# Numerators of a linear attention as 64-column products, with sums moved behind the transposes

## The chip, the core and the metric

One Trainium2 chip, one of its cores. The metric is the device time of one execution in microseconds. The kernel before took 926.39 us (median of three runs, 924.83 to 926.86). The profile that is read below is one execution of 926.11 us.

## What is computed

The reference is a FAVOR attention (4 batches, 8 heads, 576 tokens, head size 64, 128 features) followed by two feed-forward blocks on its 2304 x 512 output:

```
phi(x) = exp(x @ omega.T - |x|^2/2 - max) / sqrt(128)      # x = q or k, scaled
kv  = einsum('bhsm,bhsd->bhmd', phi(k), v)
z   = sum over tokens of phi(k)
num = einsum('bhsm,bhmd->bhsd', phi(q), kv)
den = einsum('bhsm,bhm->bhs', phi(q), z) + 1e-6
x   = num / den, heads side by side            # (2304, 512)
x   = silu(x @ w_in) @ w_out
out = (silu(x @ w_gate) * (x @ w_val)) @ w_out2
```

Everything is float32. The change touches only the attention.

## The kernel before

**Units and steps.** The attention runs over 8 units. A unit is a pair of heads and two batches, 1152 tokens in 9 chunks of 128. Each chunk is a step, so there are 72 steps and two more that finish. Two batches of 576 tokens meet inside chunk 4 of each unit: its first 64 tokens belong to one batch and its last 64 to the other.

**What a step does.** In step s, `proj` (L755 to L757) makes the features of chunk s+1 for k and q in six products of 256 columns, in one of five PSUM banks that are used in turn (`bank`). `soft` takes the maxima on VectorE (L765) and four exponentials on ScalarE (L769, tile `kq`). `kv_tr` works on the chunk of two steps ago (`LAG = 2`): it adds phi(k).T @ [v, 1] into the sums of the batch (L789, one product of 65 columns for each head), and transposes phi(q) on TensorE (L805), which ScalarE copies to `qp` (L816).

**Numerators.** When a batch's sums are complete, VectorE copies them to `st` (L826). Numerators are made for groups of three chunks (`num`, L843): for each chunk and head, one product whose weights are 128 columns of `qp` (the tokens) and whose moving operand is `st` (65 columns: the numerator and its denominator). In chunk 4 the 128 tokens belong to two batches, so that chunk already is done as products of 64 weight columns, first two for the lower half of the partitions and then two for the upper half. VectorE divides (L855 to L858), TensorE transposes the result (L868), VectorE copies it out (L877).

**When.** `tail` sets numerators two and six steps after the sums end: with u the unit, group 0 in step 9u+8, group 1 in 9u+12, group 2 in 9u+16. In step 70 there are two groups. The last two groups are made by `last_nums` when the feed-forward phase has begun. That is 24 calls: 20 in steps of their own, 2 in step 70, 2 in `last_nums`.

**Order of the work.** Every engine works through its instructions in the order in which the program issues them. Between the steps' own work, `feed` puts operations that prepare the feed-forward phase: weights of double precision turned into float32 pairs (`conv`), and operands split into high and low parts (`x`). Its choice depends on step numbers, not on times. So VectorE, ScalarE and GpSimd have a fixed list of work for each step. A projection waits until the exponentials that read its bank last are done, and `kv_tr` waits for the exponentials of its chunk.

A float32 product shows in the trace as two weight loads and two matmuls; a product of `fp32r` operands as one each.

Of the kernel before, what the change touches and what calls it, by code (L numbers as in the profile page):

```python
# [42 lines left out]
def kernel(  # L43
# [13 lines left out]
    nc = tc.nc  # L57
    ctx.enter_context(tc.manual_schedule())
    P = 128
    DM, NT = outT.shape  # L60
    D, M = omT.shape
# [12 lines left out]
    VH = D + 1  # L74
# [594 lines left out]
    def bank():  # L669
        rot.append(rot.pop(0))  # L670
        return ps[rot[-1]].rearrange("p (a b) -> p a b", a=2)
# [10 lines left out]
    raw, hl, kq, qp, kvps = {}, {}, {}, {}, {}  # L682
    v_t = [vp.tile([P, NCH, VW], F32, name=f"v{i}") for i in range(2)]
# [8 lines left out]
    def runs(lo, hi):  # L692
        for b in range(lo // S, (hi - 1) // S + 1):
            a, z = max(lo, b * S), min(hi, (b + 1) * S)
            yield b, a - lo, z - lo, a == b * S, z == (b + 1) * S
# [83 lines left out]
    def kv_tr(s):  # L779
        u, c = divmod(s, NCH)  # L780
        e = kq[s]
        ended = []
        for b, a, z, first, last in runs(c * P, (c + 1) * P):
            if first:
                kvps[u, b] = px.popleft()
            acc = ps[kvps[u, b]]
            for h in range(2):
                o = h * VH
                nc.tensor.matmul(  # L789
                    acc[:, o : o + VH],  # L790
                    e[a:z, 0, h * M : (h + 1) * M],
                    v_t[u % 2][a:z, c, o : o + VH],
                    start=first and h == 0,
                    stop=last,
                    skip_group_check=True,
                )
            if last:
                ended.append(b)
        if c == 0:
            qp[u] = ap1.tile([P, 2, UT], F32, tag="qp", name="qp", bufs=2)  # L800
        if c % 2 == 0:
            tps[u] = bank()
        t = tps[u]
        for h in range(2):
            nc.tensor.transpose(  # L805
                t[:, h, (c % 2) * P : (c % 2 + 1) * P], e[:, 1, h * M : (h + 1) * M], ident
            )
        kq.pop(s)
        if c % 2 == 1 or c == NCH - 1:
            c0 = (c - c % 2) * P  # L810
            n = (c + 1) * P - c0
            o = qp[u][:, :, c0 : c0 + n]
            if False:
                dve_q.append(lambda: nc.vector.tensor_copy(o, t[:, :, :n]))
            else:
                act_q.append(lambda: nc.scalar.activation(o, t[:, :, :n], AF.Copy))  # L816
        return [(u, b) for b in ended]

    st = {}
# [15 lines left out]
    def num(u, g, to=None):  # L835

        pxs[u, g] = x = px.popleft() if to is None else to
        acc = ps[x]
        for c in range(g * GC, (g + 1) * GC):
            for b, a, z, _, _ in runs(c * P, (c + 1) * P):  # L840
                for h in range(2):
                    o = (c - g * GC) * VW + h * VH
                    nc.tensor.matmul(  # L843
                        acc[a:z, o : o + VH],
                        qp[u][:, h, c * P + a : c * P + z],
                        st[u, b][:, h * VH : (h + 1) * VH],
                        start=True,
                        stop=True,
                        skip_group_check=True,
                    )  # L850

    def divide(u, g):
        acc = ps[pxs[u, g]][:, : GC * VW].rearrange("p (c w) -> p c w", w=VW)
# [37 lines left out]
    later = {}  # L891
# [4 lines left out]
    def tail(u, b, s):  # L896
        if b and u == NU - 1:
            return
        for g, a in ((1, s + 2), (2, s + 6)) if b else ((0, s + 2 - (u == NU - 1)),):
            at(a, num, u, g)  # L900
            at(a, lambda g=g: dve_q.append(lambda: divide(u, g)))
            at(a + 2, turn, u, g)
            at(a + 2, lambda g=g: dve_q.append(lambda: take_out(u, g)))
            if g == GC - 1:
                at(a + 4, store, u)
# [5 lines left out]
    LAG = 2  # L911

    def step(s):
# [21 lines left out]
        if LAG <= s < NSTEP + LAG:  # L935
            for ub in kv_tr(s - LAG):
                kv_evac(*ub)
                tail(*ub, s)
# [55 lines left out]
    def last_nums():  # L994

        u = NU - 1
        num(u, 1, 7)
        num(u, 2, 6)
        divide(u, 1)
        divide(u, 2)  # L1000
        nc.scalar.activation(silu, silu, AF.Silu)
        clk["PE"] += 1.8
        clk["ACT"] = max(clk["ACT"], clk["PE"]) + 1.5
        clk["DVE"] = max(clk["DVE"], clk["PE"]) + 2.0
        actx.close()
        operands("rb")
        streams["x"].extend(to_come.pop(0)())
        later_on.append((5, lambda: last_turn(1)))
        later_on.append((7, lambda: last_turn(2)))
# [632 lines left out]
```

## Time and profile before

| | |
|---|---|
| median of three runs | 926.39 us |
| profiled execution, its own time | 926.11 us |
| its span, first to last instruction | 924.3 us |
| TensorE busy (matmul) | 905.0 us, 98% |
| VectorE busy | 657.7 us, 71% |
| ScalarE busy | 558.4 us, 60% |
| GpSimd busy | 197.0 us, 21% |
| attention: last step's products end | about 146 us |

The span is shared by the attention (to about 146 us) and the two feed-forward blocks. Busy shares over the whole span hide that the other engines are much fuller in the attention than later. Matmuls are pipelined and their modelled ends overlap, so the time that a stream of products takes is read from the distance of the starts of the weight loads (PEld), not from the duration of one.

### The profile page before, as it was taken

What the parts mean: (1) busy time and instruction counts of PE and PEld (TensorE: products, weight loads), DVE (VectorE), ACT (ScalarE), POOL (GpSimd) and SP (SyncE); (2) the same over time, 40 slices, a digit from 0 to 9 for tenths busy, and PEclk for the clock granted to TensorE, in tenths of its full rate; (3) what the DMA queues carried; (4) which work ended last, traced back from release to release, by engine and by line L of the source; (5) the groups of instructions that cost most, each with busy time, mean ns of one, the idle gap of its engine ahead of it and who ended that gap; (6) DMA issues with size and microseconds to landing.
All of it is one profiled execution on the core that took longest, in us unless ns stands there. A gap on an engine that the chain in (4) does not pass through costs nothing.

```text
span 924.3 us, 15768 instructions
## 1 busy us (share of the span) xinstructions
PE 905.0 (98%) x5591; PEld 895.3 (97%) x5591; DVE 657.7 (71%) x1055; ACT 558.4 (60%) x1190; POOL 197.0 (21%) x244
## 2 busy tenths in 40 slices
PE   8999999999999998999999999999999999999998
PEld 8999999999999998999999899999999999899998
DVE  4898986857574398586689899574747447968584
ACT  5788785876667675455457765554455447445453
POOL 6676951104343100000000014221303010000000
PEclk9999999999999999999999999999999999999999
DMA  7576515848989991715613755562626159371701
GB/s 218 183 235 208 174 50 197 271 157 275 317 291 358 349 382 58 232 55 163 206 43 109 244 164 187 174 201 79 213 68 222 47 184 314 114 240 52 237 16 69
DMA packets 109888, 169.94 MB, mean 184 GB/s; under 512 B 9200, under 2 KB 93808, under 8 KB 109808
## 3 DMA queue, kind: packets, MB, share of 16 engines
q1 hardware_dynamic: 108640, 168.33, 55.8%
q8 instruction: 44, 0.72, 0.3%
q10 hardware_dynamic: 1168, 0.59, 0.2%
q14 instruction: 36, 0.29, 0.1%
HBM read 107.02 MB, written 61.87 MB: 183 GB/s over the span
## 4 chain that ended last, share of the span: by engine, by line
PE 90%; DVE 4%; DMA 3%; ACT 2%; issue 1%; SPq 0%; DVEq 0%; ACTq 0%
PE ps L1066 43%; PE ps L1433 31%; PE ps L843 3%; PE ps L789 3%; PE ps L755 2%; PE ps L756 2%; PE ps L757 2%; PE ps L805 2%; DMA g_d<-fa 1%; PE ps L868 1%; DVE ra L1296 1%; DMA fa<-in_moe_w_in 1%; DVE ra L419 0%; DMA ra<-wu_val 0%; DVE fa L1124 0%
## 5 line engine op out<-in xcount | busy, mean ns | idle before, releaser
L376 POOL TENSOR_TENSOR fa<-fa 128x256 f32<-128x256 f32 x136 | 112.6, 841 | 529.0 <-DVE fa L357 301.3
L1066 PE MATMUL ps<-ra 128*128 128x384 f32 x840 | 156.3, 335 | 3.0 <-ACT ps L1083 3.0
L1066 PE MATMUL ps<-rb,ra 128*128 128x384 f32 x840 | 157.3, 340 | 0.0
L1066 PE MATMUL ps<-rc,ra 128*128 128x384 f32 x840 | 156.8, 339 | 0.0
L1066 PEld LDWEIGHTS ps<-ra 128*128 128x128 f32 x840 | 146.7, 188 | 4.3 <-ACT ps L1083 4.3
L1066 PEld LDWEIGHTS ps<-rb,ra 128*128 128x128 f32 x840 | 148.7, 188 | 0.3 <-ACT ps L1083 0.3
L1066 PEld LDWEIGHTS ps<-rc,ra 128*128 128x128 f32 x840 | 148.6, 188 | 0.1
L1083 ACT ACTIVATE ps<-ps 128x384 f32<-128x384 f32 x180 | 85.5, 476 | 88.7 <-PE ps L1066 82.1
L1140 DVE TENSOR_TENSOR fa<-fa,ps 128x384 f32<-128x384 f32 x120 | 66.2, 552 | 100.5 <-ACT ps L1083 78.1
L1292 ACT ACTIVATE ra<-fa 128x768 fp32r<-128x768 f32 x105 | 88.0, 844 | 81.2 <-PE ps L1433 64.4
L1296 DVE TENSOR_TENSOR ra<-fa,ra 128x768 fp32r<-128x768 f32 x105 | 100.5, 957 | 50.5 <-PE ps L1433 31.9
L1433 PE MATMUL ps<-ra,rb 128*128 128x384 f32 x720 | 129.4, 340 | 0.0
L1433 PEld LDWEIGHTS ps<-ra,rb 128*128 128x128 f32 x720 | 127.8, 189 | 0.8 <-DVE ra L1296 0.6
L1433 PE MATMUL ps<-ra 128*128 128x384 f32 x612 | 109.7, 337 | 6.7 <-DVE ra L1296 6.5
L1433 PEld LDWEIGHTS ps<-ra 128*128 128x128 f32 x612 | 106.7, 189 | 8.8 <-DVE ra L1296 8.0
L769 ACT ACTIVATE kq<-ps,nb 128x128 f32<-128x128 f32 x288 | 83.1, 403 | 25.3 <-DVE nb L765 24.1
L1433 PE MATMUL ps<-ra,rc 128*128 128x384 f32 x432 | 78.2, 340 | 1.6 <-DVE ra L1296 1.6
L1433 PEld LDWEIGHTS ps<-ra,rc 128*128 128x128 f32 x432 | 76.1, 188 | 2.7 <-DVE ra L1296 2.7
L1107 ACT ACTIVATE fa<-fa 128x384 f32<-128x384 f32 x84 | 43.8, 522 | 28.8 <-DVE fa L1140 28.5
L1316 DVE TENSOR_TENSOR fa<-ra,fa 128x768 f32<-128x768 f32 x63 | 60.1, 954 | 0.7
L1292 ACT ACTIVATE ra<-ra 128x768 fp32r<-128x768 f32 x42 | 35.5, 845 | 36.0 <-PE ps L1433 32.1
L1296 DVE TENSOR_TENSOR ra<-ra 128x768 fp32r<-128x768 f32 x42 | 40.2, 958 | 20.9 <-PE ps L1433 9.3
(100 smaller groups left out, 1227.6 us busy)
## 6 DMA issues: line engine op xcount, KB each, us to landing
g_d<-fa SPq DMA_DIRECT2D x168, 192.0 KB, 3.4
fa<-g_d SPq DMA_DIRECT2D x42, 384.0 KB, 4.4
ra<-g_d SPq DMA_DIRECT2D x42, 384.0 KB, 4.1
fa<-in_moe_w_out SPq DMA_DIRECT2D x28, 512.0 KB, 5.3
fa<-in_moe_w_in SPq DMA_DIRECT2D x16, 512.0 KB, 5.0
wd_out<-fa SPq DMA_DIRECT2D x14, 512.0 KB, 3.3
fa<-in_moe_w_gate SPq DMA_DIRECT2D x12, 512.0 KB, 3.9
fa<-in_moe_w_val SPq DMA_DIRECT2D x12, 512.0 KB, 5.2
```

The source lines that it names most:

```text
L376: f(blk(f"S{n}"), blk(l), blk(r))
L769: nc.scalar.activation(e[:, i, h * M : (h + 1) * M], ps[:, i, h * M : (h + 1) * M], AF.Exp, bias=nb[:, 2 * i + h : 2 * i + h + 1],)
L789: nc.tensor.matmul(acc[:, o : o + VH], e[a:z, 0, h * M : (h + 1) * M], v_t[u % 2][a:z, c, o : o + VH], start=first and h == 0, stop=last, ...
L843: nc.tensor.matmul(acc[a:z, o : o + VH], qp[u][:, h, c * P + a : c * P + z], st[u, b][:, h * VH : (h + 1) * VH], start=True, stop=True, sk ...
L1066: nc.tensor.matmul(ps[b][:, :N], cut(l, j * P, P), cut(r, j * N, N), start=start and c == 0, stop=stop and c == 5, skip_group_check=True,)
L1083: nc.scalar.activation(out() if callable(out) else out, src, AF.Copy)
L1107: nc.scalar.activation(b["t"], src, AF.Silu)
L1140: nc.vector.tensor_add(t, t if in_place else p5[n], ps[bank_][:, :N])
L1292: nc.scalar.activation(ops[s, p, k][0], src(), AF.Copy)
L1296: nc.vector.tensor_sub(l, src(), h.bitcast(F32))
L1316: (nc.gpsimd if eng == "POOL" else nc.vector).tensor_sub(z(PLACE[to]), z(PLACE.get(l, l)), z(PLACE.get(r, r)))
L1433: nc.tensor.matmul(ps[BANKS[p] + e][:, :N], cut(a, e * P, P), b, start=p in FIRST and i == 0 and c == 0, stop=p in LAST and i == fp - 1 an ...
```

## The change

In `num` each product of 128 weight columns becomes two of 64, one that writes the lower half of the partitions and one that writes the upper half. In those steps that make numerators, the sums of k and v (the same products as before, otherwise of 128 weight columns) are made in halves of 64 columns as well, and are issued after the transposes, directly ahead of the numerators. Steps without numerators keep their sums as they were, and `last_nums` changes through `num` alone.

```
@@ kv_tr
+        halves = any(f is num for f, _ in later.get(s + LAG, ()))
+        then = None
...
-            for h in range(2):
-                o = h * VH
-                nc.tensor.matmul(
-                    acc[:, o : o + VH],
-                    e[a:z, 0, h * M : (h + 1) * M],
-                    v_t[u % 2][a:z, c, o : o + VH],
...
+            def sums(w, a=a, z=z, first=first, last=last, acc=acc):
+                for h in range(2):
+                    o = h * VH
+                    for i in range(0, M, w):
+                        nc.tensor.matmul(
+                            acc[i : i + w, o : o + VH],
+                            e[a:z, 0, h * M + i : h * M + i + w],
+                            v_t[u % 2][a:z, c, o : o + VH],
...
+            if halves:
+                then = sums
+            else:
+                sums(M)
...            (the transposes)
+        if then:
+            then(D)
@@ num
                     o = (c - g * GC) * VW + h * VH
-                    nc.tensor.matmul(
-                        acc[a:z, o : o + VH],
-                        qp[u][:, h, c * P + a : c * P + z],
+                    for i in range(a, z, D):
+                        nc.tensor.matmul(
+                            acc[i : i + D, o : o + VH],
+                            qp[u][:, h, c * P + i : c * P + i + D],
```

TensorE, the first step with a group 0: `v` and `kq` are the sums' operands, `ident` those of the transposes, `st` and `qp` those of the numerators; each row is a product before it is taken apart into two instructions.

```order
-L789 MATMUL ps_84<-v_98,kq 128x65 x2
-L805 MATMUL ps_81<-ident,kq 128x128 x2
-L843 MATMUL ps_85<-st,qp 128x65 x6
+L814 MATMUL ps_81<-ident,kq 128x128 x2
+L793 MATMUL ps_84<-v_98,kq 64x65 x4
+L855 MATMUL ps_85<-st,qp 64x65 x12
```

The transposes stand first, and the eight products of 128 weight columns have become sixteen of 64 in one row.

TensorE, the first step with a group 1, which holds chunk 4; the two products of the next projection follow.

```order
-L789 MATMUL ps_83<-v_99,kq 128x65 x2
-L805 MATMUL ps_81<-ident,kq 128x128 x2
-L843 MATMUL ps_84<-st,qp 128x65 x2
-L843 MATMUL ps_84<-st,qp 64x65 x4
-L843 MATMUL ps_84<-st,qp 128x65 x2
+L814 MATMUL ps_81<-ident,kq 128x128 x2
+L793 MATMUL ps_83<-v_99,kq 64x65 x4
+L855 MATMUL ps_84<-st,qp 64x65 x12
 L755 MATMUL ps_78<-om_hi,hik 128x256
 L756 MATMUL ps_78<-om_hi,lok 128x256
```

Before, four products of 64 columns stood between products of 128; now all sixteen are of 64, and the step after begins as it did. On VectorE, ScalarE, GpSimd and the DMA queues the order is the same in both kernels.

## Rows read from the trace of the kernel before

**Rows 1.** The page's first part: busy us (share of the span) and instructions.

```profile
PE 905.0 (98%) x5591; PEld 895.3 (97%) x5591; DVE 657.7 (71%) x1055; ACT 558.4 (60%) x1190; POOL 197.0 (21%) x244
```

**Rows 2.** The chain of waits, 0 to 146 us, shares by line.

```profile
by line: PE ps L789 20.5%; PE ps L843 19.9%; PE ps L755 12.9%; PE ps L756 12.6%; PE ps L757 12.2%; PE ps L805 11.9%; PE ps L868 4.9%; DMA rawq<-in_q 2.8%; SPq L720 0.8%; DVE lok L708 0.6%; issue 0.3%; SPq L699 0.3%; PE ps L1043 0.1%; DVEq L
```

**Rows 3.** Timeline, weight loads from 72.8 us, a group 2: start us, us, what.

```profile
73.42 1.42 PEld L843 LDWEIGHTS ps<-st,qp 128*128 128x128 f32 x12
74.75 0.19 PEld L755 LDWEIGHTS ps<-om_hi,hik 128*128 128x128 f32 x1
```

**Rows 4.** Timeline, weight loads from 62.7 us, a group 1 with chunk 4.

```profile
63.34 1.50 PEld L843 LDWEIGHTS ps<-st,qp 128*128 128x128 f32 x16
64.76 0.19 PEld L755 LDWEIGHTS ps<-om_hi,hik 128*128 128x128 f32 x1
```

**Rows 5.** Groups by shape, weight loads, 0 to 150 us: count, busy us, mean ns, idle before.

```profile
L843 PEld LDWEIGHTS ps<-st,qp 128*128 128x128 f32 x256 | 31.0, 192 | 0.5
...
L843 PEld LDWEIGHTS ps<-st,qp 128*64 128x64 f32 x64 | 2.6, 136 | 0.5
```

**Rows 6.** Timeline, weight loads, 63.9 to 64.3 us: chunk 4 alone.

```profile
63.93 0.32 PEld L843 LDWEIGHTS ps<-st,qp 128*64 128x64 f32 x8
```

**Rows 7.** Timeline of weight loads from 146 us: the last numerators.

```profile
146.96 2.90 PEld L843 LDWEIGHTS ps<-st,qp 128*128 128x128 f32 x28
```

**Rows 8.** Windows of the attention: length, then busy us of PE, PEld, DVE, ACT, POOL.

```profile
30.30:79.50 49.20, 49.20 (x456) 48.32 (x454) 46.80 (x94) 39.36 (x127) 36.16 (x45) 1.00 0.60 185
79.50:104.30 24.80, 24.80 (x235) 24.12 (x233) 21.65 (x42) 19.93 (x66) 18.77 (x22) 1.00 0.68 218
104.30:146.00 41.70, 41.70 (x386) 41.02 (x385) 32.70 (x69) 32.17 (x106) 23.66 (x27) 1.00 0.26 81
```

**Rows 9.** A window from 91.94 us, the same columns as above.

```profile
91.94:104.27 12.33, 12.33 (x119) 11.99 (x117) 11.69 (x22) 9.63 (x31) 12.00 (x14) 1.00 0.50 147
```

**Rows 10.** Waits of VectorE, 30.3 to 79.5 us: total us, times, longest.

```profile
DVE rc L855 <- PE ps L843: 2.5, 4, 1.1
DVE fa L350 <- ACT fa L343: 0.2, 1, 0.2
```

**Rows 11.** Timeline of all engines from 78.0 us, two rows.

```profile
77.76 0.67 ACT L769 ACTIVATE kq<-ps,nb 128x128 f32<-128x128 f32 x2
...
79.42 0.37 PE L755 MATMUL ps<-om_hi,hik 128*128 128x256 f32 x1
```

**Rows 12.** Timeline of VectorE from 87.5 us; in brackets the idle time before.

```profile
87.94 0.43 DVE L350 TENSOR_SCALAR fa<-fa 128x512 uint32<-128x512 uint32 x1 [0.81 <-ACT fa L343]
...
89.75 0.16 DVE L855 TENSOR_SCALAR rc<-ps 128x6 f32<-128x6 f32 x1 [0.79 <-PE ps L843]
...
92.43 0.16 DVE L855 TENSOR_SCALAR rc<-ps 128x6 f32<-128x6 f32 x1 [0.49 <-PE ps L843]
```

**Rows 13.** Timeline of all engines from 103.8 us, two rows.

```profile
103.50 0.63 ACT L769 ACTIVATE kq<-ps,nb 128x128 f32<-128x128 f32 x2
...
104.27 0.36 PE L755 MATMUL ps<-om_hi,hik 128*128 128x256 f32 x1
```

**Rows 14.** Timeline of all engines from 130.5 us, two rows.

```profile
130.18 0.88 ACT L769 ACTIVATE kq<-ps,nb 128x128 f32<-128x128 f32 x3
...
131.72 0.36 PE L755 MATMUL ps<-om_hi,hik 128*128 128x256 f32 x1
```

**Rows 15.** Timeline of VectorE from 147 us: the last divisions.

```profile
148.70 0.17 DVE L855 TENSOR_SCALAR rc<-ps 128x6 f32<-128x6 f32 x1 [2.49 <-PE ps L843]
...
150.04 0.16 DVE L855 TENSOR_SCALAR rc<-ps 128x6 f32<-128x6 f32 x1 [0.36 <-PE ps L843]
...
150.47 0.56 DVE L858 TENSOR_TENSOR nt<-ps,rc 128x384 f32<-128x384 f32 x1
```

**Rows 16.** The chain of waits from 130 us, in order of time: its end.

```profile
156.42 6.09 DMA fa<-in_moe_w_in
...
164.03 96.12 PE ps L1066 x545
```

More of the change, by code (lines that the diff above doesn't have):

```diff
@@ L786, in kv_tr @@
             acc = ps[kvps[u, b]]
-            for h in range(2):
-                o = h * VH
-                nc.tensor.matmul(
-                    acc[:, o : o + VH],
-                    e[a:z, 0, h * M : (h + 1) * M],
-                    v_t[u % 2][a:z, c, o : o + VH],
[L793 to L796, printed above, removed]
+            def sums(w, a=a, z=z, first=first, last=last, acc=acc):
[6 more added lines that the diff above has]
+                            v_t[u % 2][a:z, c, o : o + VH],
+                            start=first and h == 0,
+                            stop=last,
+                            skip_group_check=True,
+                        )
+            if halves:
+                then = sums
+            else:
+                sums(M)
             if last:
@@ L842, in num @@
                     o = (c - g * GC) * VW + h * VH
-                    nc.tensor.matmul(
-                        acc[a:z, o : o + VH],
-                        qp[u][:, h, c * P + a : c * P + z],
[L846 to L850, printed above, removed]
+                    for i in range(a, z, D):
+                        nc.tensor.matmul(
+                            acc[i : i + D, o : o + VH],
+                            qp[u][:, h, c * P + i : c * P + i + D],
+                            st[u, b][:, h * VH : (h + 1) * VH],
+                            start=True,
+                            stop=True,
+                            skip_group_check=True,
+                        )
     def divide(u, g):
```

## The prediction, made before the changed kernel ran

> **What bounds the kernel now.** I read the page's first part, the chain of waits over the attention, the weight loads of TensorE by shape and in time, and the windows of the attention for the other engines. Over the whole span TensorE is busy 98% of the time and the others at most 71% [rows 1]. In the first 146 us the chain lies on TensorE's lines almost alone: the sums (L789) hold 20.5% of it and the numerators (L843) 19.9%, each nearly twice a projection line [rows 2]. So what a step takes is what TensorE needs for it, and the question has two halves: how much shorter the changed products make TensorE's own work, and how long the other engines can follow.
>
> **TensorE's own work.** A product of 65 moving columns is paced by its weight load. In a step with a group 2, twelve instructions of 128 weight columns start at 73.42 and the next projection's load at 74.75 us [rows 3]: 1.33 / 12 = 0.111 us for each, sums included, since they have the same shape. A group 1 holds eight of these and the eight 64-column instructions of chunk 4, and takes 64.76 - 63.34 = 1.42 us [rows 4]; less 8 x 0.111 = 0.89, chunk 4 costs 0.53 us with everything around it. A load of 64 columns lasts 136 ns on average [rows 5], yet all eight are over in 0.32 us [rows 6]. One after another at the half of 0.111 us they would need 7 x 0.056 + 0.136 = 0.53 us. They go in pairs, one for each half of the partitions: (0.32 - 0.136) / 3 = 0.06 us from pair to pair. So a pair of halves, which does the work of one 128-column instruction, costs 0.06 instead of 0.111 us, and going into this shape and out of it costs 0.53 - 4 x 0.06 = 0.29 us once.
>
> This is where a rule speaks against the change. The Trainium skill, TensorE: Matmul & The Clock Gate, "The mechanism", says that a weight load overlaps matmuls in flight only when the row group differs; these halves use all rows, so they would gain nothing. The trace disagrees by rows 6. The Trainium skill, TensorEngine Tiling (Array Packing), "Key Properties", says that changing the tiling mode drains the engine but that tiles load and multiply in parallel; the 0.29 us and the pairs are what that looks like here.
>
> Step by step, with n instructions of 128 columns before and n pairs after, the block costs 0.29 + 0.06n:
> - Thirteen steps with a group 0 or 2: 12 numerators and 4 sums, 16 x 0.111 = 1.78 us before, 0.29 + 0.96 = 1.25 after. Gain 0.53 us each, 6.9 in sum. If the sums had stayed as 128 columns, the gain would be 0.32.
> - Seven steps with a group 1: (8 + 4) x 0.111 + 0.53 = 1.86 before, 1.25 after; 0.61 each, 4.3 in sum.
> - Step 70, with two groups: 28 x 0.111 = 3.11 before, 1.97 after; 1.14.
> - The last two groups, no sums: 20 x 0.111 + 0.53 = 2.75 (28 weight loads, busy 2.90 with the last one's tail [rows 7]), 1.73 after; 1.0.
>
> Together 13.3 us of TensorE's time; with 0.056 us for a pair it would be 14.3. The transposes that move ahead of the sums cost nothing: same instructions, and ScalarE gets them earlier. The sums of those steps are never the ones that end a batch, so their later place delays no copy.
>
> **How far the others follow.** The other engines keep their lists of work. From 30.3 to 79.5 us VectorE is busy 46.80 of 49.20 us, and GpSimd is busy 12.00 of 12.33 us later on [rows 8, 9]. VectorE's maxima feed the exponentials, and a projection must wait until those that read its bank are done. So TensorE can be ahead of its old schedule by no more than the exponentials' lead plus the slack that the old schedule had there. I call the gained time "lead" and follow it by stretches.
> - To 30.3 us: one group 0 and one group 1, lead 1.14 us. VectorE idles enough to follow.
> - To 79.4 us: TensorE would gain six of 0.53 and two of 0.61, to a lead of 5.5. VectorE can gain only what it idles. It waits for numerators 2.5 us, of which 1.1 is the wait that ends at the window's start, and 0.2 for ScalarE [rows 10]: 1.4 to 1.6, so its lead is 2.55 to 2.75. At 79.42 a projection starts 0.99 us after the exponentials of 77.76 + 0.67 end [rows 11]. TensorE's lead is cut to 2.75 + 0.99 = 3.75; 1.8 us are lost.
> - To 104.3 us: gains of 2 x 0.61 + 2 x 0.53 = 2.3 would make it 6.0. VectorE waits 0.81 for ScalarE, which lags itself and gives back nothing, then 0.79 and 0.49 for numerators [rows 12]: its lead is 3.5 to 4.0. From 92 us GpSimd is 97% busy, too, and hands work to VectorE, so I take 3.65, near the lower end. At 104.27 a projection starts only 0.14 us after the exponentials end (103.50 + 0.63) [rows 13]. The lead here is 3.8, which loses another 2.2.
> - To 146 us: VectorE has 9 us of idle time, busy 32.70 of 41.70 [rows 8], and follows. Gains 4 x 0.53 + 2 x 0.61 + 1.14 = 4.5. One narrow place: 131.72 against 131.06, 0.66 us [rows 14], after two groups close together of which VectorE has caught up with half: 0.3 lost. Lead 8.0.
> - The last numerators: the first division starts 0.5 us earlier (half of the 1.0), at 148.2 instead of 148.70. The two divisions take 1 us each (150.47 + 0.56 - 150.04) and stand back to back, so the end at 151.03 comes to 150.2: 0.8 us [rows 15].
>
> Behind that nothing eats the lead: the load of 6.09 us for which the first feed-forward phase waits until 164.03 us [rows 16] is issued behind the last result's store, so it moves along with the attention's end.
>
> The sum is 3.8 + 4.5 - 0.3 + 0.8 = 8.8 us. From the profiled execution's 926.11 us that gives 917.3; the median of the runs is 0.28 us above that execution, so I predict 917.6 us. Bounds of the uncertain terms: VectorE's lead at 104 us between 2.75 (no gain after 79.4) and 5 (ScalarE holds nothing) moves the sum from 7.9 to 10.1, and 0.056 us for a pair adds 0.4 in the last stretches: 915 to 920 for this case.
>
> **Rivals.**
> - The others follow fully. VectorE's busy time contains waits that would pass in less time, or the exponentials are later than their readers need. For it: TensorE is at no point shown to wait for them now. Against it: 95% and a slack of 0.14 us. All 13.3 to 14.3 us come through: 912 to 913.
> - The others hold harder. ScalarE is busy 80% in the first two windows of rows 8 as well; once TensorE no longer sets the beat, each late operation of VectorE, ScalarE and GpSimd delays the next, where I added up only the tightest places. A gain of 2 to 6 us: 920 to 924.5.
> - The halves run one after another (slower). Chunk 4 issued all products of the lower half and then all of the upper; now they alternate, product by product, and a queue that holds the upper half back until the lower is done would undo the pairs. Then a step's 32 loads take 32 x 0.06 + 0.29 = 2.21 us against 1.78: 13 x 0.43 + 7 x 0.35 + 0.54 + 0.42 = 9.0 us more on TensorE, which is the bound: 935. It decides once a pair takes over 0.093 us, where 16 of them cost (1.78 - 0.29) / 16. Against it: in rows 6 four loads of the lower half stood ahead of the first of the upper, which still ran beside them. By the row-group rule named above this would be the outcome.
> - The change does little: pairs overlap in part, at about 0.09 us, and the entry and exit cost eat the rest: 926.
>
> **Chances.** Forecast 0.55, full gain 0.17, harder hold 0.17, serial halves 0.06, little 0.05. What a measurement here can tell from no change is 0.2%, 1.9 us. Slower by that takes the serial halves and a share of the last case, 0.07; within it 0.03; faster 0.90. The range for 8 in 10 goes from 912.3, inside the full gain, to 921.5, inside the harder hold.
>
> **What would show it.** In the changed profile a step with a group 0 or 2 should show the weight loads of sums and numerators in about 1.25 us, and loads of 64 columns in pairs. If it shows 1.25 us and the total is near 912, VectorE did not hold; then TensorE still has no idle time before 146 us. By my forecast TensorE should now wait at projections for the exponentials (L769), some 4 to 5 us in sum, most of it between 50 and 100 us, and VectorE should hardly wait for numerators there. The prediction fails if that block takes 2 us, or if TensorE's waits in the attention are under 2 or over 8 us.

## Result and profile after

The changed kernel takes 917.45 us (median of 4 runs, 916.33 to 918.47) against 925.95 us for the kernel before (4 runs). The ratio is 0.9903, 95% interval 0.9884 to 0.9922: 8.5 us faster, with 7.2 to 10.7 us inside the interval, where 8.8 was the forecast. The profiled execution of after took 918.47 us, the longest of its four, so against the one before (926.11 us) its trace shows 7.6 us.

The page's first part of after (busy us, share of the span, instructions); it answers to [rows 1].

```profile
PE 895.6 (98%) x5931; PEld 879.3 (96%) x5931; DVE 657.0 (72%) x1055; ACT 557.9 (61%) x1190; POOL 198.3 (22%) x244
```

TensorE's share is still 98%, so the page hides what happened; the other engines have the same work as before.

The timeline of weight loads in a step with a group 1 of after (start us, us, what, idle before); it answers to [rows 4].

```profile
59.59 0.19 PEld L757 LDWEIGHTS ps<-om_lo,hiq 128*128 128x128 f32 x1
59.73 0.24 PEld L814 LDWEIGHTS ps<-ident,kq 128*128 128x128 f32 x2
60.14 0.32 PEld L793 LDWEIGHTS ps<-v,kq 128*64 128x64 f32 x8 [0.17 <-issue]
60.37 0.83 PEld L855 LDWEIGHTS ps<-st,qp 128*64 128x64 f32 x24
61.27 0.19 PEld L755 LDWEIGHTS ps<-om_hi,hik 128*128 128x128 f32 x1
```

32 loads of 64 columns go from 60.14 to 61.27, 1.13 us for 16 pairs, though one load still lasts about 137 ns. Ahead of them stands a gap of 0.17 us that no wait explains.

Who held TensorE's weight loads from 7 to 150 us in after (us in total, times, longest).

```profile
PEld ps L793 <- issue: 3.5, 21, 0.2
PEld ps L755 <- ACT kq L769: 2.0, 4, 1.2
...
PEld ps L1055 <- DVE nt L870: 1.1, 1, 1.1
PEld ps L755 <- POOL fa L601: 0.6, 1, 0.6
PEld ps L880 <- DVE nt L870: 0.6, 2, 0.5
...
PEld ps L855 <- DVE st L837: 0.2, 1, 0.2
```

The first row is the gap ahead of the 21 blocks. Before, this view shows one wait, 0.9 us for `lok`. The rows with kq, fa, nt (L880) and st are new: projections, transposes and numerators now wait for the other engines. Only 2.0 us of this name the exponentials, in four waits; the prediction expected 4 to 5 us there.

Windows of after that answer to [rows 8] and [rows 9] (from and to, length, then busy us of PE, PEld, DVE, ACT, POOL).

```profile
30.60:75.05 44.45, 44.04 (x554) 40.73 (x553) 43.70 (x85) 36.34 (x117) 34.42 (x42) 1.00 0.62 198
...
86.03:104.16 18.13, 16.70 (x209) 15.17 (x206) 17.90 (x34) 13.80 (x46) 15.58 (x18) 1.00 0.49 152
```

VectorE has gone from 95% to 98% of the first window and is busy 99% of the second, while TensorE, never idle before, lacks 1.4 us in the second. The waits of VectorE from 30 to 75 us in after, against [rows 10]:

```profile
DVE fa L350 <- ACT fa L343: 0.2, 1, 0.2
```

It no longer waits for a numerator. From 69 to 75 us the chain of waits of after lies on VectorE where TensorE stands still (start us, us, what):

```profile
70.05 0.94 DVE fa L350
70.99 0.60 DVE nb L765
...
71.92 0.56 DVE nt L870
72.47 0.60 DVE fa L357
73.07 0.60 DVE nb L765
```

Maxima (L765) and divisions are what TensorE needs; L350 and L357 are weight conversions of the feed-forward phase that stand between them in VectorE's order.

The end of the attention, weight loads, first before (the rows behind those of [rows 7]), then in after.

```profile
149.78 0.19 PEld L1043 LDWEIGHTS ps<-ra 128*128 128x128 f32 x1
151.08 0.19 PEld L1043 LDWEIGHTS ps<-ra 128*128 128x128 f32 x1 [1.10 <-DVE nt L858]
```

```profile
140.98 1.53 PEld L855 LDWEIGHTS ps<-st,qp 128*64 128x64 f32 x48 [0.26 <-issue]
142.58 0.19 PEld L1055 LDWEIGHTS ps<-ra 128*128 128x128 f32 x1
143.91 0.19 PEld L1055 LDWEIGHTS ps<-ra 128*128 128x128 f32 x1 [1.15 <-DVE nt L870]
```

The last two groups' block went from 146.96 to 149.78 us, 2.82; it is now 140.98 to 142.58, 1.60. The load that waits for the last division (`nt`) started at 151.08 and now starts at 143.91: the attention ends 7.2 us earlier, and the divisions still end it.

### The profile page after: what moved, and what is told of

Read it like the earlier page. It is cut to its first block, busy times and chain, and to the rows that moved or that the text cites. A ratio compares the mean times of both kernels' runs of the same rounds, so it can differ in the third digit from the quotient of the medians.

```text
span 916.7 us, 16448 instructions
## 1 busy us (share of the span) xinstructions
PE 895.6 (98%) x5931; PEld 879.3 (96%) x5931; DVE 657.0 (72%) x1055; ACT 557.9 (61%) x1190; POOL 198.3 (22%) x244
## 4 chain that ended last, share of the span: by engine, by line
PE 81%; DVE 7%; DMA 5%; ACT 2%; issue 2%; POOL 1%; SPq 0%; DVEq 0%; ACTq 0%; POOLq 0%
PE ps L1078 42%; PE ps L1445 31%; PE ps L793 2%; PE ps L755 1%; DMA g_d<-fa 1%; PE ps L756 1%; PE ps L757 1%; PE ps L855 1%; PE ps L814 1%; POOL fa L376 1%; DMA v<-in_v 1%; DVE nb L765 1%; DVE ra L1308 1%; DVE ra L419 1%; DMA x_d<-xt 1%
```

## Experiments

"The stretch" below goes from the start of the tenth projection, which stands at the head of step 8, to that of the seventy-first, at the head of step 69: 20.22 to 137.46 us in the kernel before, 117.2 us; 20.50 to 132.28 us in after, 111.8 us. It holds all twenty steps with one group: thirteen with a group 0 or 2 and seven with a group 1. The length of a step is the distance between the starts of two projections.

**E1. Numerators in halves, sums as before.**

```
-        halves = any(f is num for f, _ in later.get(s + LAG, ()))
+        halves = False
```

Expected: 

> Numerators in halves, sums of 128 columns ahead of the transposes as before. From the changed kernel's trace a block of pairs costs 0.40 us for going in and out and 0.058 us for a pair. Theory (TensorE gains by that price, and the other engines hold back what they cannot follow): 12 pairs cost 1.10 us against 1.33 before, so TensorE gains 13 x 0.24 + 7 x 0.32 + 0.9 + 0.9 = 7.1 us, and little of it is held back since the lead stays near 3 us where VectorE is full: 918.9 to 919.6 us. Rival (nothing is held back; the whole 8.5 us that the change gave are TensorE's own, in proportion): 8.5 x 7.1 / 11.6 = 5.2 us, 920.7 us.

Measured: 918.59 us (918.25 to 919.49), ratio 0.9922 [0.9902, 0.9942]. That is 7.3 us where the theory had 7.1, and 0.3 us under the range that I had written down; the rival's 920.7 lies above all runs. The weight loads of a step with a group 1:

```profile
61.34 0.26 PEld L814 LDWEIGHTS ps<-ident,kq 128*128 128x128 f32 x2
61.77 0.83 PEld L855 LDWEIGHTS ps<-st,qp 128*64 128x64 f32 x24 [0.17 <-issue]
62.67 0.19 PEld L755 LDWEIGHTS ps<-om_hi,hik 128*128 128x128 f32 x1
```

12 pairs from 61.77 to 62.67 us, 0.90; with the 1.13 for 16 pairs, (1.13 - 0.90) / 4 = 0.058 us is the price of a pair. One projection still waits 1.2 us for its exponentials, in step 52. Halving the sums too makes a step with a group 0 shorter by 0.16 us (2.36 here, 2.19 in after) and 21 steps by 3.4, but brought only 1.1 us in the medians and 0.7 in the stretch (112.5 here): the rest was held back.

**E2. Sums in halves, but ahead of the transposes.**

```
-            if halves:
-                then = sums
-            else:
-                sums(M)
+            sums(D if halves else M)
```

Expected: 

> Both in halves, but the sums ahead of the transposes, so that 64-column products, 128-column transposes and 64-column products follow each other. Theory (each block of 64 columns costs 0.40 us for going in and out): 0.40 us more in each of 21 steps, so TensorE gains 11.6 - 8.4 = 3.2 us and nothing is held back: 922 to 923 us; the step with a group 0 takes about 2.6 us. Rival (the change of shape is free, the pairs alone count): as the changed kernel, 917.5 us.

Measured: 920.05 us (918.54 to 921.9), ratio 0.9939 [0.9918, 0.9959]; between theory and rival. The weight loads of a step with a group 1:

```profile
61.76 0.19 PEld L757 LDWEIGHTS ps<-om_lo,hiq 128*128 128x128 f32 x1
62.08 0.32 PEld L793 LDWEIGHTS ps<-v,kq 128*64 128x64 f32 x8
62.47 0.20 PEld L811 LDWEIGHTS ps<-ident,kq 128*128 128x128 f32 x2
62.84 0.83 PEld L852 LDWEIGHTS ps<-st,qp 128*64 128x64 f32 x24 [0.17 <-issue]
63.73 0.19 PEld L755 LDWEIGHTS ps<-om_hi,hik 128*128 128x128 f32 x1
```

From the projection's last load to the next projection 1.97 us, where after takes 1.68: a second block costs 0.29 us, not the 0.40 that I expected. That makes 21 x 0.29 = 6.1 us of TensorE's time, of which 2.6 reach the total, because here again less is held back. The stretch agrees: 115.0 us, 3.2 more than in after, as 20 steps take 5.9 more and 2.7 less is held back. So the move behind the transposes is worth having, and the change of shape is not free.

**E3. Half by half.** All numerators of a group for the lower half, then all for the upper.

```
-        for c in range(g * GC, (g + 1) * GC):
+        for half in (0, D):
+          for c in range(g * GC, (g + 1) * GC):
...
-                    for i in range(a, z, D):
+                    for i in (range(half, half + D, D) if a <= half < z else ()):
```

Expected: 

> Numerators in halves, all of a group for the lower half of the partitions first, then all for the upper half (12 loads, then 12); sums as in the changed kernel. Theory (the two halves have queues of their own, and chunk 4 showed 4 loads ahead of the other half without loss): as the changed kernel, 917.5 us within 0.5. Rival (TensorE looks only so far ahead that the order, half after half of each product, is what makes the pairs): the 12 pairs of a group become up to 24 loads in a row, 0.7 us more in each of 24 groups, 16 us on TensorE: 926 to 932 us.

Measured: 924.91 us (923.73 to 927.15), ratio 0.9991 [0.9978, 1.0005]: the gain is gone. The theory's 917.5 fell, and the rival's 926 to 932 was not quite reached. Windows of one block, numerators' instructions alone (length, busy us and count of PE and of PEld; a load that crosses a border counts twice):

```profile
64.05:64.57 0.52, 0.46 (x8) 0.51 (x9) 1.00 0.98 256
64.57:64.80 0.23, 0.23 (x10) 0.23 (x9) 1.00 1.12 296
64.80:65.30 0.50, 0.50 (x15) 0.50 (x11) 1.00 1.05 312
```

Nine loads take 0.52 us one after another, 0.058 us each, the next go side by side for 0.23 us, and then the upper half's rest is alone for 0.50. So the other half starts beside the last three of the twelve that stand ahead of it. Alone, a load of 64 columns takes as long as a pair of them, and half of the 0.111 us of one of 128 with the same 65 moving columns: the weight columns set the pace. This is in part what my prediction's slower rival said, made real by another order; its full price, every load alone and 935 us, did not come.

**E8. Four ahead.** In each chunk both heads of the lower half, then both of the upper.

```
-            for b, a, z, _, _ in runs(c * P, (c + 1) * P):
-                for h in range(2):
+            for i, h in ((0, 0), (0, 1), (D, 0), (D, 1)):
+                for b, a, z, _, _ in runs(c * P, (c + 1) * P):
...
-                    for i in range(a, z, D):
+                    if a <= i < z:
```

Expected: 

> Numerators of each chunk as four instructions for the lower half, then four for the upper (both heads of one half first). E3 showed that with twelve ahead the other half starts only nine loads later. Theory (TensorE starts the other half about three products ahead of its place, so four loads ahead are no loss, as in chunk 4 of the kernel before): steps with a group 0 take 2.19 us as in the changed kernel, 917.5 us. Rival (only strict alternation runs side by side): over 2.4 us in such a step, 920 us or more.

Measured: 918.11 us (917.19 to 918.59), ratio 0.9913 [0.9897, 0.9929], not to be told from after. A step with a group 0 takes 2.24 us, against 2.19 in after and 2.67 before: with four loads ahead nearly everything runs in pairs. (In chunk 4, where two batches meet, the changed kernel has this order itself.) Strict alternation isn't needed; twelve ahead is too far.

**E4 and E5. No feed-forward work in the attention**, in the kernel before and in the changed one.

```
-            if s >= 8:
+            if s >= 999:
...
-            if s >= 27:
+            if s >= 999:
```

Expected of e4: 

> The kernel before, with no operation of the feed-forward phase put between the attention's steps (all of them run after the attention). The total is longer for that alone and is not the point: read is the attention, from the tenth projection to the seventy-first. Both theories: as before with the feed, 117.2 us, since TensorE was the bound there: 9 steps take 17.4 us.

Expected of e5: 

> The changed kernel without those operations in the attention. Theory (VectorE, ScalarE and GpSimd, full with the feed-forward phase's operations, hold TensorE back): every unit of 9 steps takes 16.0 us, no projection waits for exponentials, and the same stretch takes 108 us, 9 us less than e4; with the feed it was 111.8 against 117.2, only 5.5 less. Rival (the waits are the attention's own: maxima, exponentials, divisions): about 111.5 us, waits of 3 to 4 us as in the changed kernel.

Measured: 971.96 and 957.69 us in all (2 runs each), as the work then stands behind the attention. The ends of the stretch, a timeline of TensorE, in before, after, e4 and e5:

```profile
20.22 0.36 PE L755 MATMUL ps<-om_hi,hik 128*128 128x256 f32 x1
...
137.46 0.36 PE L755 MATMUL ps<-om_hi,hik 128*128 128x256 f32 x1
```

```profile
20.50 0.36 PE L755 MATMUL ps<-om_hi,hik 128*128 128x256 f32 x1
...
132.28 0.36 PE L755 MATMUL ps<-om_hi,hik 128*128 128x256 f32 x1
```

```profile
20.82 0.36 PE L755 MATMUL ps<-om_hi,hik 128*128 128x256 f32 x1
...
138.00 0.36 PE L755 MATMUL ps<-om_hi,hik 128*128 128x256 f32 x1
```

```profile
20.50 0.36 PE L755 MATMUL ps<-om_hi,hik 128*128 128x256 f32 x1
...
128.30 0.36 PE L755 MATMUL ps<-om_hi,hik 128*128 128x256 f32 x1
```

The stretch is 117.2 us in e4 and 107.8 in e5: 9.4 us less, where the change gave 5.5 with the feed (117.24 - 111.78). The waits of weight loads in e5 from 7 to 139 us show no exponentials and no divisions within the steps:

```profile
PEld ps L793 <- issue: 3.5, 21, 0.2
PEld ps L1055 <- issue: 3.5, 1, 3.5
PEld ps L756 <- DVE lok L708: 1.2, 1, 1.2
...
```

So 111.8 - 107.8 = 4.0 us are held back in after, and it is the fed work that holds them. The attention's own maxima, exponentials and divisions would have kept up.

**E6 and E7. VectorE's fed work spread**, at most one operation in a step and none in every ninth; the two lines of `feed` change places.

```
+            k = 0 if s % NCH in (0,) else 1
+            left = sum(o.eng == "DVE" for q in early.values() for o in q)
+            if s >= 27:
+                feed("x", s, {"SP": 4, "ACT": 2, "DVE": k, "POOL": 1})
+            k -= left - sum(o.eng == "DVE" for q in early.values() for o in q)
             if s >= 8:
-                feed("conv", s, {"SP": 1, "ACT": 1, "DVE": 1, "POOL": 1})
-            if s >= 27:
-                feed("x", s, {"SP": 4, "ACT": 2, "DVE": 2, "POOL": 1})
+                feed("conv", s, {"SP": 1, "ACT": 1, "DVE": max(k, 0), "POOL": 1})
```

Expected of e6, on the kernel before: 

> The kernel before, with VectorE's fed operations spread: at most one in a step, none in every ninth, so that the 48 operations end in step 69 and not in step 64. Theory (TensorE alone is the bound there): no change, 925.9 us within 0.7. Rival (spreading is a gain of its own): 923 or less.

Expected of e7, on the changed kernel: 

> The changed kernel, with the same spreading. Theory (others hold back 3.7 us because VectorE's fed operations lie close in steps 13 to 63): two thirds of the waits go, 914.5 to 916 us; what remains is in steps 48 to 53, where GpSimd is full. Rival (the waits are not VectorE's load but transfers and GpSimd, which the spreading leaves): 917 to 918 us.

Measured: e6 925.97 us, ratio 0.9997 [0.9987, 1.0008], no change, as the theory has it. e7 916.61 us (915.87 to 916.97), ratio 0.9899 [0.9883, 0.9915]: short of the expected 914.5 to 916, and its 0.8 us against after are within the spread of the runs. The trace tells more: the stretch takes 110.6 us, 1.2 less than in after. Step by step against e5, only 0.15 us is left in the steps where after lost its 4.0 (34 to 44 and 50 to 53), though nothing but VectorE's share of the feed and the order of the two lists was changed; so this points to VectorE's fed work there, and not to GpSimd, which I had expected to go on holding in steps 48 to 53. But the waits moved: e7 loses 0.6 us shortly before and 2.0 in steps 61 to 66. Its chain from 90 to 104 us goes over a store of converted weights to GpSimd.

```profile
92.08 7.59 DMA wd_out<-fa
99.67 0.03 issue
...
99.81 1.07 POOL fa L376
100.88 0.49 POOL hik L706
```

**E9 and E10. The storing job last.** The job whose results go to DRAM stands behind the other three: e9 with e7's spreading; e10 with two steps of nine left out (`k = 0 if s % NCH in (0, 4) else 1`, and `k` for VectorE in both lines of `feed`, so at most two operations in the other steps).

```
-chain(conv_job("in", 0), conv_job("in", 1), down_job(0, 0), conv_job("in", 2))
+chain(conv_job("in", 0), conv_job("in", 1), conv_job("in", 2), down_job(0, 0))
```

Expected of e9: 

> E7 (VectorE's fed operations spread) with the one weight job whose results go to DRAM moved behind the other three. In E7 the projections of steps 61 to 65 waited for splits on GpSimd, 2.0 us, and the chain went to the store of that job (7.6 us to landing), which GpSimd's next sums wait for. Theory (that store set GpSimd's place): these waits go, 914.5 to 915.5 us. Rival (GpSimd is simply full there): as e7, 916.6 us.

Expected of e10: 

> The changed kernel with the same order of jobs, and VectorE's fed operations left out only in the two steps of nine in which a division stands beside no numerators (step numbers 0 and 4 modulo 9); up to two in other steps from step 27 on. Theory (the peak of VectorE's load between steps 13 and 40 decides): between e9 and the changed kernel, 915 to 916.5 us, waits in steps 34 to 41 reduced from 2 to under 1 us. Rival (the sum of the load counts, not its place): 917 us.

Measured: e9 914.42 us (913.17 to 916.08), ratio 0.9877 [0.9854, 0.9900]; e10 914.65 us (913.42 to 915.89), ratio 0.9877 [0.9859, 0.9895]. Both are about 3 us better than the changed kernel and the fastest of the study: the longest run of either is shorter than the shortest of the changed kernel, though the intervals of the ratios overlap a little, and the stretch is shorter than in after by 2.5 us in e9 and 3.1 in e10. For e9 I expected 914.5 to 915.5, for e10 915 to 916.5. From e7 to e9 only the order of the jobs changed, and e7's late loss is gone with it (0.4 us in step 59 are left of 2.0). The new order without a spreading was not run on the changed kernel. The waits in e10, weight loads from 7 to 139 us:

```profile
PEld ps L793 <- issue: 3.5, 21, 0.2
PEld ps L756 <- DVE lok L708: 1.2, 1, 1.2
PEld ps L755 <- ACT kq L769: 0.7, 1, 0.7
...
```

One wait for exponentials is left, 0.7 us; the stretch takes 108.6 us (20.43 to 129.07), 0.8 above e5, with all the fed work in it.

**E11. E10's order in the kernel before.** Expected: 

> The kernel before with e10's order of jobs and e10's skipped steps. Theory (TensorE is the bound in the attention of the kernel before, so where the others' work lies makes no difference there): 925.9 us within 0.8. Rival (the order of jobs gains in its own right, there or in the feed-forward phase): 923.5 us or less, as much as e10 gained over the changed kernel.

Measured: 925.94 us, ratio 0.9997 [0.9986, 1.0007]. The order that gives the changed kernel 3 us gives the kernel before nothing: there TensorE was the bound.

## Why the prediction was right

**The pairs: right.** A pair costs 0.058 us, with 0.06 predicted; one load of 128 columns cost 0.111 before. E3 shows that this hangs on the order, as the slower rival said; the order of the change is on the safe side, and E8 shows that it has room. The Trainium skill, TensorE: Matmul & The Clock Gate, "The mechanism", says that a weight load overlaps matmuls in flight only when the row group differs. By that rule no order could have gained; the trace does not agree, as here 32 loads on all rows take 1.13 us.

**TensorE's gain: too large by about a sixth.** I took the price of going in and out, 0.29 us, from chunk 4, where 64-column products stand between other numerators. After transposes there are 0.17 us of idle time ahead of each block. From the transposes' first load to the next projection a group 1 takes 61.27 - 59.73 = 1.54 us, of which 0.23 belong to the transposes: the block costs 1.31 us where I had 1.25, and 1.31 - 16 x 0.058 = 0.38 us for in and out. The first group 0 takes 22.69 - 21.20 = 1.49 us between the same two loads: 1.26 for the block and 0.33 for in and out, nearly what I had. The rest of the difference lies outside the block: the old sums took 0.40 us for four loads and not 0.44, and the transposes, now directly behind the projection, start 0.03 us later than the sums did. From the first weight load of one projection to that of the next, a step with a group 0 or 2 went from 2.67 to 2.22 us and one with a group 1 from 2.76 to 2.27: gains of 0.45 and 0.49, for 0.53 and 0.61 predicted. (The starts of the products, used above, give 2.19 and 2.24 in after and put the difference into the steps beside.) In the stretch that makes 9.4 us (e4 against e5) for the 13 x 0.53 + 7 x 0.61 = 11.2 that my terms give.

**The hold: right in place and cause, its size in part by luck.** I had 1.8 us lost by 79.4 us, 2.2 more by 104.3 and 0.3 later, 4.3 in all. Step by step against e5, after loses 1.9 us in steps 34 to 44 (66 to 86 us of its trace; 1.4 of it by the projection that started at 79.42 before), 2.1 in steps 50 to 53 (to 104 us), and nothing later: 4.0 us, in the 4 to 5 that the prediction named. The 0.3 at 131.72 us did not come; why was not tried. E5 shows the fed work as the cause, and e7 points to VectorE's part of it in both places. The rule that VectorE's lead plus the slack of the next reader limits TensorE's lead held, too. The exponentials and the projections of [rows 11] and [rows 13] in after:

```profile
75.76 0.67 ACT L769 ACTIVATE kq<-ps,nb 128x128 f32<-128x128 f32 x2
76.48 0.39 PE L755 MATMUL ps<-om_hi,hik 128*128 128x256 f32 x1
...
100.70 1.14 ACT L769 ACTIVATE kq<-ps,nb 128x128 f32<-128x128 f32 x4 [0.76 <-DVE nb L765]
101.90 0.39 PE L755 MATMUL ps<-om_hi,hik 128*128 128x256 f32 x1 [1.01 <-ACT kq L769]
```

The exponentials, which follow VectorE's maxima, end 2.0 us earlier than before (76.43 for 78.43) and 2.3 us earlier (101.84 for 104.13). With the old slack of 0.99 and 0.14 us that allows leads of 3.0 and 2.4; the projections are 2.9 and 2.4 us earlier. But I had VectorE 2.75 and 3.65 us ahead, and so TensorE 3.75 and 3.8: its idle time was not all gained. 0.3 us of each difference is the later start of after's stretch. Another part shows in the row that stood at 87.94 us before with 0.81 us of idle time, a conversion that follows ScalarE; in after it waits longer:

```profile
85.88 0.43 DVE L350 TENSOR_SCALAR fa<-fa 128x512 uint32<-128x512 uint32 x1 [1.51 <-ACT fa L343]
```

What else VectorE lost is open. What is lost is TensorE's own gain less the lead that it may have, and I had both too large by about the same, 1.3 and 1.2 us by 104 us counted from the start of the stretch; so the loss came out at 4.0 by 104 us where 3.9 were measured.

**The last groups: right.** From the start of the seventy-second projection, at the head of step 70, to the load behind the last division it takes 143.91 - 133.97 = 9.9 us where it took 151.08 - 139.14 = 11.9: 2.0 us for step 70 and the last block, 1.14 + 0.8 predicted.

**The sum.** 5.5 (the stretch) + 2.0 = 7.5 us; the stretch begins 0.3 us later than before (20.50 against 20.22), which leaves the 7.2 us by which the attention ends earlier, where I had 8.8. The first feed-forward phase adds 0.7, as its load took 5.33 us and not 6.09, and 0.3 are lost later; the span is 7.6 us shorter. The medians differ by 8.5 us, as the profiled execution of after lies 1.0 us above its kernel's median and that of before 0.2 above its own. So the forecast was nearer to the medians than its terms were to the trace, and that is luck: of the 13.3 us that I had for TensorE 11.4 came (9.4 in the stretch and 2.0 behind it), and of the 4.3 us that I let the others hold back 4.0.

What stays open: why the block idles 0.17 us behind transposes but less behind numerators, why VectorE's lead grew so little between 79 and 104 us, and what the later phases add: e9's stretch is 0.6 us longer than e10's, yet its profiled span is 1.8 us shorter (912.3 and 914.1), and the medians are the same.

## What to carry to other kernels

When one engine sets the beat, a change that shortens its work gains only up to the idle time of the next engine plus the slack of whoever waits; add that up stretch by stretch ahead of the change. Then look for work that shares the next engine and can stand elsewhere: here it was worth nothing before the change and about 3 us after it (e11 against e10). Products that load 128 weight columns for few moving columns (here 65) are paced by the load, and two halves on different output partitions cost about half (0.058 us for 0.111), if the halves stand near each other in the order; each block of them costs 0.3 to 0.4 us for going in and out, so make it long. When a forecast is the difference of two terms, check the terms in the trace and not their difference alone.

## What I had not expected of the hardware

The reach of TensorE's overlap between the halves. Four loads of one half ahead of the other cost 0.05 us in a step (2.24 against 2.19 in e8), twelve ahead undid the gain: nine of them ran alone for 0.52 us (e3). And a change between 128 and 64 weight columns has a price that depends on what stands before it: 0.29 us for a second block (e2), 0.33 to 0.38 for the block behind transposes.
